# Keeping the first token block's x on chip, and 24 instead of 16 tiles with scores masked in PSUM, in a fused attention and two-MLP kernel

## The chip, the core and the metric

The kernel runs on one core of a Trainium2 chip. The metric is device time in microseconds (us) of one execution. The engines are TensorE (PE, matrix multiplications; PEld is its weight load), VectorE (DVE), ScalarE (ACT), GpSimd (POOL) and SyncE (SP, which issues the DMAs here). Each engine works through its own instructions in the order in which they were written.

## The reference

All inputs are float32. Attention has 4 batches, 8 heads, 576 tokens and 64 numbers for each head; the two MLPs then work on 2304 tokens of width 512.

```python
scores = (q @ k.T) / sqrt(64)
thresh = max(scores) - tau                     # for each row of scores
e = exp(where(scores >= thresh, scores, -1e9) - max(scores))
x = (e / (sum(e) + 1e-9)) @ v                  # (2304, 512) after the heads are put side by side
h = x @ w_in;  y = (h * sigmoid(h)) @ w_out    # 512 -> 2048 -> 512
out = ((y @ w_a) * (y @ w_b)) @ w_o            # 512 -> 1536 -> 512
```

## The kernel before

**Order of work.** The whole program is a list of tasks (`pl.add`), each with an engine, an estimated cost, a rank, the tasks that it needs, and the buffers that it takes (`take`) and gives back (`pl.free`). A list scheduler (`Plan.run`) plays the tasks through with the estimated costs and writes each engine's instructions in the order in which they start there. So the order is fixed when the kernel is built, by estimates; on the chip an instruction whose operands come late holds up everything behind it on its engine. A buffer ring such as `hb=1` has so many buffers, and its takers come in the order in which the tasks were added. Where the plan sees PE idle ahead of a transposition, `turn` puts in up to 16 transpositions that serve nothing else (L558).

**Attention.** Two heads are a pair (`c` = 0 to 3), and the queries of a batch come in two halves of 256 and 320 tokens. A tile is 128 query rows against all 576 keys. The first batch goes through all pairs with its first half (tiles 0 to 15, 4 for each pair), then through all pairs with its second half (tiles 16 to 35, 5 for each); the other batches follow. For each tile (`softmax`): PE computes the scores into a PSUM buffer, "sa" or "sb" (L502); DVE scales them and finds the extreme of each row (`lowest`, L511); a small DVE instruction makes the threshold; ACT takes the exponential (L523 or L525); DVE masks it and sums each row (`mask`, L528). `weigh` then turns the tile with PE transpositions in pieces of 128 columns (L560, into "tp" or "hb"), ACT copies them to SBUF (L567), and for each pair and half PE multiplies with `v` into the PSUM tile "av" (L605).

**Early tiles.** A tile with number below `EARLY` = 16 alternates between "sa" and "sb", its exponential and its mask read the scores from PSUM, and the buffer comes free with the mask. The transpositions of tiles below `EARLY - 2` use "hb" for every third piece of work. A later tile uses "sa" alone: `lowest` writes the scaled scores to SBUF as well (tile "t"), the exponential and the mask read "t", and "sa" comes free after `lowest`.

**The sums.** `inverses` adds a small number to the 4 or 5 columns of row sums (`guard`, L457) and takes their reciprocals (`inverse`, L460) into one shared tile "sums". PE transposes "sums" into the same "av" bank (`turn_sums`, L610). ACT copies both to SBUF (`evacuate`, L626, tile "x", ring of one). A DMA stores the inverse sums to DRAM (L630), a second one loads them back spread over the partitions (L637, "xi"), POOL multiplies (`divide`, L640), and a third DMA stores x to DRAM (L644).

**The MLPs.** The first MLP works on token blocks: five of 256 tokens, then two of 512. Block 0 is the first half of batch 0. `load_x` reads x of a block from DRAM for each pair (L694, "xr"), ACT rounds it to float32r (L699, "xh") and POOL takes the rest (L702, "xl"). `mlp1_up` and `mlp1_down` go over 16 chunks f of the inner width, PE in the order up(0), up(1), down(0), and so on. `up` accumulates in "hb" (L730), `down` of the first blocks in "sb" (L790); ACT and DVE apply the gate between them (L740, L743, L746, L749). Attention has the better rank on PE. The weights of the first MLP come in 32 chunks of 512 KB (L326), one for every 1.3 tiles; ACT, DVE and POOL split each one (L330, L335, L341, L346, L350, L354, L358). The second MLP follows (L876, L920).

Of the kernel before, what the change touches and what calls it, by code (L numbers as in the profile page):

```python
# [20 lines left out]
B, H, S, D = 4, 8, 576, 64  # L21
P = 128
# [9 lines left out]
TB = 256  # L32

BLOCKS = tuple((i * TB, TB) for i in range(5)) + ((5 * TB, 512), (5 * TB + 512, 512))
# [11 lines left out]
R_T, R_AV, R_EV, R_NORM = 2, 3, 1, -2  # L46
R_LD, R_SPLIT, R_AUX, R_MLP = -9, -6, -1, 1000

SPLIT_FROM = 54

EARLY = 16

AV_PARTS = ((0, 1, 2, 3), (4,))

# [6 lines left out]
PIECE = 128  # L61
# [153 lines left out]
def fused_kernel(ctx: ExitStack, tc: tile.TileContext, qk, qk2, v, tau, w_in, w_out, w_a, w_b, w_o2, out):  # L215
# [9 lines left out]
    nc = tc.nc  # L225
    pl = Plan()
# [8 lines left out]
    def pool(stack, name, bufs, side="left", **kw):  # L235
# [18 lines left out]
    xb_p = pool(p1, "xb", RINGS["xb"])  # L254
# [7 lines left out]
    x_p = pool(att, "x", RINGS["x"])  # L262
# [6 lines left out]
    sums = const.tile([P, P], F32, name="sums")  # L269
# [5 lines left out]
    ident = const.tile([P, P], F32, name="ident")  # L275
# [113 lines left out]
    att_tasks = []  # L389

    def add(engine, cost, rank, fn, after=(), take=(), behind=(), **kw):
        t = pl.add(engine, cost, rank, fn, after, take, behind, **kw)
        att_tasks.append(t)
        return t
# [51 lines left out]
        att_tasks.append(s["ready"])  # L446
        return s

    def inverses(n, m):

        s = {}

        def guard():
            nc.vector.tensor_scalar(out=s["sum"][:, :m], in0=s["sum"][:, :m], scalar1=EPS, scalar2=None, op0=ALU.add)  # L457

        def inverse():
            nc.vector.reciprocal(out=sums[:, :m], in_=s["sum"][:, :m])  # L460

        def total(k):
            def fn():
                if "sum" not in s:
                    s["sum"] = sm_p.tile([P, 5], F32, name="sum", bufs=2)
                return s["sum"][:, k:k + 1]
            return fn

        def finish(masked):
            gd = add("DVE", 150, n + R_NORM, guard, masked)  # L470
            return add("DVE", 150, n + R_NORM, inverse, [gd], ["rs"])

        return total, finish

    counter = [0]

# [69 lines left out]

    def weigh(b, half, c, tiles, v, last):

        q0, nq = HALVES[half]
        buf = "pb" if half else "pa"  # L550
        s = {}

# [15 lines left out]
            return fn  # L568

        left, full, es = [], [], []  # L570
        total, finish = inverses(counter[0] + len(tiles), len(tiles))

        def move(r, chunks, dst, *free):
            t = {"bank": "hb" if r < EARLY - 2 and turns[0] % 3 == 2 else "tp"}
# [13 lines left out]
        for n, parts in enumerate(tiles):  # L588
            e = softmax(parts, total(n))
            es.append(e)  # L590
            r = first + n
            tn = move(r, [(e, k * P) for k in range(4)], lambda p, n=n: p[:, :4, n * P:(n + 1) * P])
            if n % 2 or n == len(tiles) - 1:

                m = n % 2 + 1
                tn = move(r, [(x, S - P) for x in es[-m:]], lambda p, n=n, m=m: p[:, 4, (n + 1 - m) * P:(n + 1) * P])
                for _ in range(m):
                    pl.free("e", tn)
        last_n = first + len(tiles) - 1
# [7 lines left out]

        def turn_sums():
            s["av"] = ps_av.tile([P, 512], F32, name="av")
            nc.tensor.transpose(s["av"][:, nq:nq + P], sums, ident)  # L610

        iv = finish([e["ready"] for e in es])
        ts = add("PE", 110, last_n + R_AV, turn_sums, [iv], ["av"])
        pl.free("rs", ts)

        av = ts
        for ks in AV_PARTS:
            av = add("PE", 2 * len(ks) * (int(nq / 1.2) + 47) + 100, last_n + R_AV, lambda ks=ks: values(ks),
                     [*(left if 4 in ks else full), v["ready"]], behind=[av])
# [2 lines left out]
            pl.free("v", av)  # L622

        def evacuate():
            s["x"] = x_p.tile([P, 320 + P], F32, name="x")
            nc.scalar.copy(out=s["x"][:, :nq + P], in_=s["av"][:, :nq + P])  # L626

        def store_sums():
            k0 = 4 * half
# [7 lines left out]
            nc.sync.dma_start(out=s["i"][:, :nq], in_=r.broadcast_to((2, D, nq)))  # L637

        def divide(o):
            nc.gpsimd.tensor_tensor(out=s["x"][:, o], in0=s["x"][:, o], in1=s["i"][:, o], op=ALU.mult)  # L640

        def store():
            t0 = b * S + q0
            nc.sync.dma_start(out=xT_d[c, :, t0:t0 + nq], in_=s["x"][:, :nq])  # L644

        ev = add("ACT", act_ns(nq + P, True), last_n + R_EV, evacuate, [av], ["x"])
        pl.free("av", ev)
        st = dma(-1, 5 * P * 4, store_sums, after=[ev], slack=500)
        ld = dma(-1, P * 4 * nq, load_sums, after=[st], take=["xi"], slack=SLACK)
        dv = on_pool(nq, last_n + R_EV, divide, [ld], PIECE)  # L650
# [26 lines left out]
    xs, gs, ys = {}, {}, {}  # L677
    x_ready, g_ready, w_last = {}, {}, {}
    up_last, down_last, y_dma, b_done = [None], [None], [], []

    def load_x(j):
        s = xs[j] = {}
        t0, tn = BLOCKS[j]
        big = tn > TB
        x_p = lambda: pools["b5"] if big else xb_p
        ring, raw = ("x5", "xr5") if big else ("xb", "xr")

        def split(c):
            need = [t for (b, half, heads), ts in x_dma.items() for t in ts
                    if heads == c and b * S + HALVES[half][0] < t0 + tn and b * S + sum(HALVES[half]) > t0]  # L690

            def load():
                s["r", c] = x_p().tile([P, tn], F32, name=raw, bufs=RINGS[raw])
                nc.sync.dma_start(out=s["r", c], in_=xT_d[c, :, t0:t0 + tn])  # L694

            def hi():
                s["h", c] = x_p().tile([P, tn], F32R, name="xh5" if big else "xh", bufs=RINGS[ring])
                s["l", c] = x_p().tile([P, tn], F32R, name="xl5" if big else "xl", bufs=RINGS[ring])
                nc.scalar.copy(out=s["h", c], in_=s["r", c])  # L699

            def lo(o):
                nc.gpsimd.tensor_tensor(out=s["l", c][:, o], in0=s["r", c][:, o], in1=s["h", c][:, o].bitcast(F32), op=ALU.subtract)  # L702

            ld = dma(-1, P * 4 * tn, load, after=need, take=[raw], slack=SLACK, behind=[closed] if big else [])
            h = pl.add("ACT", act_ns(tn), R_AUX, hi, [ld], [ring])
            l = on_pool(tn, R_AUX, lo, [h], PIECE)[-1]
            pl.free(raw, l)
            x_ready[j, c] = (h, l)

        for c in range(NC):  # L710
            split(c)
# [260 lines left out]
    closed = pl.add("none", 1, 0, close_attention, behind=[*att_tasks, *closed0])  # L972
    units = [(j, f) for j in range(len(BLOCKS)) for f in range(NF)]
    for n, u in enumerate(units):
        if u[1] == 0:
            load_x(u[0])
        mlp1_up(n, *u)
        if n:
            mlp1_down(n - 1, *units[n - 1])
# [76 lines left out]
```

## Time and profile before

| | us |
|---|---|
| median of 3 runs | 1173.22 (1172.68 to 1173.97) |
| the profiled execution | 1174.95 |
| its span, first to last instruction | 1173.2 |
| PE busy in it | 1142.9 (97%) |
| DVE, ACT, POOL busy | 621.7, 531.1, 271.4 |

The span is what the rows below are taken from; the time of the same execution is 1.75 us above it. A busy time is the time in which an engine had an instruction in work; idle time in a row is the time the engine stood just before an instruction, and "<-" names what ended it. [...]

### The profile page before, as it was taken

The page shows a single profiled execution, that of the slowest core. Times are in us where ns is not written, and L with a number is a line of the kernel's source. Part 1 is how long each engine was busy: PE and PEld are TensorE (multiplying, and loading weights), DVE is VectorE, ACT ScalarE, POOL GpSimd, SP SyncE. Part 2 cuts the span into 40 slices and gives each one's busy share as a digit, 9 for nine tenths or more (in the row PEclk, how much of TensorE's full clock was granted, in tenths as well). Part 3 has the DMA queues.
Part 4 walks back from the last instruction along what each step waited for, and adds up shares of the span by engine and source line. Part 5 has one row for each costly group of instructions (what it writes and reads, how often), then busy time and mean ns, then how long its engine had stood idle before and what let it go on. Part 6 is the DMA issues. An engine that isn't in the chain of part 4 may idle for free.

```text
span 1173.2 us, 18253 instructions
## 1 busy us (share of the span) xinstructions
PE 1142.9 (97%) x6917; PEld 957.8 (82%) x6917; DVE 621.7 (53%) x1416; ACT 531.1 (45%) x999; POOL 271.4 (23%) x440
## 2 busy tenths in 40 slices
PE   8789989999999999999999999999999999999998
PEld 6456757988999989899888888888888888888897
DVE  8988887877777777463223678673211311211121
ACT  7877786666766766442223445442211211211121
POOL 2444444333322422140001344451000000000000
PEclk9999999999999999999999999999999999999999
DMA  6654543322322221150001235440100200000000
GB/s 199 199 163 138 163 155 109 113 88 79 107 73 84 82 95 35 36 190 18 1 1 45 88 111 167 140 138 13 63 1 1 68 0 1 23 28 1 1 36 18
DMA packets 41095, 90.05 MB, mean 77 GB/s; under 512 B 4256, under 2 KB 18224, under 8 KB 41008
## 3 DMA queue, kind: packets, MB, share of 16 engines
q1 hardware_dynamic: 40864, 88.89, 23.7%
q8 instruction: 54, 0.88, 0.3%
q14 instruction: 33, 0.27, 0.1%
q10 hardware_dynamic: 144, 0.00, 0.0%
HBM read 74.65 MB, written 14.23 MB: 76 GB/s over the span
## 4 chain that ended last, share of the span: by engine, by line
PE 60%; DMA 2%; DVE 1%; ACT 1%; issue 0%; POOL 0%; SPq 0%; ACTq 0%; POOLq 0%
PE ps_a L876 13%; PE op L920 13%; PE ps_b L876 13%; PE hb L730 5%; PE hc L730 4%; PE sb L790 3%; PE yc L790 2%; PE yd L790 1%; PE ye L790 1%; PE yf L790 1%; DMA wraw<-w_a 1%; PE av L605 1%; PE tp L560 1%; PE sa L495 1%; DMA wraw<-w_b 1%
## 5 line engine op out<-in xcount | busy, mean ns | idle before, releaser
L886 DVE TENSOR_TENSOR z<-ps_b,z 128x512 f32<-128x512 f32 (+1 forms) x60 | 38.2, 637 | 227.9 <-PE ps_b L876 227.8
L730 PE MATMUL hb<-xh,w 128*128 128x256 f32 (+1 forms) x704 | 155.2, 310 | 1.5 <-DVE th L743 1.0
L350 POOL TENSOR_TENSOR wt<-wc,wt 128x128 uint32<-128x128 uint32 (+1 forms) x164 | 111.2, 702 | 140.2 <-DVE wc L346 98.7
L920 PE MATMUL op<-w,zh 128*128 128x512 f32 x432 | 133.9, 391 | 0.0
L511 DVE TENSOR_SCALAR_CACHE_REDUCE t<-sa,nscale 128x576 f32<-128x576 f32 x128 | 103.7, 810 | 50.6 <-PE sa L495 45.6
L528 DVE SCALAR_TENSOR_TENSOR e<-t,thr,e 128x576 f32<-128x576 f32 x128 | 111.5, 871 | 26.4 <-ACT e L525 24.8
L730 PEld LDWEIGHTS hb<-xh,w 128*128 128x128 f32 x704 | 113.0, 190 | 10.9 <-issue 2.3
L560 PE MATMUL tp<-ident,e 128*128 128x128 f32 x706 | 106.2, 278 | 12.9 <-DVE e L528 8.3
L560 PEld LDWEIGHTS tp<-ident,e 128*128 128x128 f32 x706 | 78.7, 140 | 37.2 <-issue 14.7
L525 ACT ACTIVATE e<-t,min 128x576 f32<-128x576 f32 x128 | 99.9, 781 | 19.2 <-DVE t L511 18.5
L883 ACT COPY z<-ps_a 128x512 f32<-128x512 f32 (+1 forms) x60 | 32.6, 543 | 165.0 <-PE ps_a L876 165.0
L730 PE MATMUL hb<-xl,w 128*128 128x256 f32 (+1 forms) x352 | 106.5, 303 | 0.7 <-POOL xl L702 0.7
L790 PE MATMUL sb<-gh,w 128*128 128x256 f32 (+1 forms) x576 | 97.6, 300 | 0.0
L920 PEld LDWEIGHTS op<-w,zh 128*128 128x128 f32 x432 | 80.3, 188 | 16.4
L889 ACT CAST zh<-z 128x512 fp32r<-128x512 f32 (+1 forms) x60 | 34.7, 578 | 127.5 <-DVE z L886 127.5
L790 PEld LDWEIGHTS sb<-gh,w 128*128 128x128 f32 x576 | 80.0, 190 | 5.9 <-issue 3.3
L920 PE MATMUL op<-w,zl 128*128 128x512 f32 x216 | 84.6, 392 | 0.0
L749 DVE TENSOR_TENSOR gl<-th,gh 128x256 fp32r<-128x256 f32 (+1 forms) x112 | 63.9, 571 | 28.3 <-ACT gh L746 28.1
L876 PE MATMUL ps_a<-yha,w 128*128 128x512 f32 (+1 forms) x288 | 77.4, 355 | 0.0
L876 PE MATMUL ps_b<-yha,w 128*128 128x512 f32 (+1 forms) x288 | 77.0, 354 | 0.0
L640 POOL TENSOR_TENSOR x<-x,xi 128x128 f32<-128x128 f32 (+2 forms) x80 | 40.9, 535 | 147.1 <-issue 49.9
L702 POOL TENSOR_TENSOR xl<-xr,xh 128x128 fp32r<-128x128 f32 x72 | 37.0, 542 | 161.0 <-ACT xh L699 156.4
(123 smaller groups left out, 2342.8 us busy)
## 6 DMA issues: line engine op xcount, KB each, us to landing
qk<-qk SPq DMA_DIRECT2D x20, 576.0 KB
wraw<-w_in SPq DMA_DIRECT2D x16, 512.0 KB
wraw<-w_out SPq DMA_DIRECT2D x16, 512.0 KB
v<-v SPq DMA_DIRECT2D x20, 320.0 KB
wraw<-w_a SPq DMA_DIRECT2D x12, 512.0 KB
wraw<-w_b SPq DMA_DIRECT2D x12, 512.0 KB
wraw<-w_o SPq DMA_DIRECT2D x12, 512.0 KB
out<-ob SPq DMA_DIRECT2D x18, 256.0 KB
```

The source lines that it names most:

```text
L350: nc.gpsimd.tensor_tensor(out=s["t"][:, o], in0=s["c"][:, o].bitcast(U32), in1=s["t"][:, o], op=ALU.add)
L511: nc.vector.tensor_scalar(out=s["t"], in0=s["s"][:, :, :NH], scalar1=nscale, scalar2=None, op0=ALU.mult, op1=ALU.min, accum_out=s["min"])
L525: nc.scalar.activation(out=s["e"], in_=s["t"], func=AF.Exp, scale=-1.0, bias=s["min"])
L528: nc.vector.scalar_tensor_tensor(out=s["e"], in0=s["s"][:, :, :NH] if early else s["t"], scalar=s["thr"], in1=s["e"], op0=ALU.is_ge if ear ...
L560: nc.tensor.transpose(t["tp"][:, j * P:(j + 1) * P], e["e"][:, o:o + P], ident)
L640: nc.gpsimd.tensor_tensor(out=s["x"][:, o], in0=s["x"][:, o], in1=s["i"][:, o], op=ALU.mult)
L730: nc.tensor.matmul(s["h"], lhsT=w[:, a, o:o + P], rhs=xx, start=(c == 0 and k == 0), stop=(c == NC - 1 and k == 2))
L749: nc.vector.tensor_sub(out=s["gl"], in0=s["t"], in1=s["gh"].bitcast(F32))
L790: nc.tensor.matmul(ys[j][e // per][:, e % per * tn:(e % per + 1) * tn], lhsT=w[:, a, e * P:(e + 1) * P], rhs=gs[j, f][g], start=(f == 0 an ...
L876: nc.tensor.matmul(s[nm][:, :tn], lhsT=w[:, a, o:o + P], rhs=yy[:, :tn], start=(c == 0 and k == 0), stop=(c == NC - 1 and k == 2))
L886: nc.vector.tensor_mul(out=s["z"][:, :tn], in0=s["b"][:, :tn], in1=s["z"][:, :tn])
L920: nc.tensor.matmul(o_ps[t0, i], lhsT=s[z][:, i * P:(i + 1) * P], rhs=wt["o2", f][:, a, :], start=(f == 0 and k == 0), stop=(f == NF2 - 1 a ...
```

## The change

For the first half of batch 0 (`stays`), x no longer goes to DRAM and back.

- `inverse` takes the reciprocal of each sum 64 times over: DVE writes a tile of 128 x 4 x 64 numbers ("xi") from the 4 sums, read with a broadcast.
- `turn_sums` is four matmuls with a 128x64 weight from that tile and the identity, in place of one transposition. They put the inverse sums of 128 queries into 64 partitions each, beside the product with `v` in the "av" bank.
- `evacuate` copies 512 columns instead of 384, and `divide` reads the inverse sums from the same tile "x".
- The DMAs L630, L637, L644 and L694 of these four pairs are gone, and with them the buffer "xr". The split into "xh" and "xl" (now `split_x`) reads the tile "x" as soon as POOL has multiplied, and "x" comes free when the split is done.
- `EARLY` is 24: tiles 16 to 23 alternate between "sa" and "sb", keep their scores in PSUM until the mask, and write no tile "t"; transpositions of tiles 14 to 21 use "hb" for every third piece of work as well. "hb" and "sb" come to the first MLP after their last takers among these tiles.

```diff
-EARLY = 16
+EARLY = 24
...
-    def inverses(n, m):
+    def inverses(n, m, wide):
...
         def inverse():
-            nc.vector.reciprocal(out=sums[:, :m], in_=s["sum"][:, :m])
+            if wide:
+                s["wide"] = x_p.tile([P, 320], F32, name="xi")[:, :m * D].rearrange("p (m d) -> p m d", d=D)
+                nc.vector.reciprocal(out=s["wide"], in_=s["sum"][:, :m].rearrange("p (m o) -> p m o", o=1).broadcast_to((P, m, D)))
+            else:
+                nc.vector.reciprocal(out=sums[:, :m], in_=s["sum"][:, :m])
...
-            return add("DVE", 150, n + R_NORM, inverse, [gd], ["rs"])
+            return add("DVE", dve_ns(m * D) if wide else 150, n + R_NORM, inverse, [gd], ["xi" if wide else "rs"])
...
         q0, nq = HALVES[half]
+        stays = b == 0 and half == 0
...
         def turn_sums():
             s["av"] = ps_av.tile([P, 512], F32, name="av")
-            nc.tensor.transpose(s["av"][:, nq:nq + P], sums, ident)
+            if stays:
+                for k in range(4):
+                    nc.tensor.matmul(s["av"][k // 2 * D:(k // 2 + 1) * D, nq + k % 2 * P:][:, :P], lhsT=inv["wide"][:, k, :], rhs=ident,
+                                     start=True, stop=True, skip_group_check=True)
+            else:
+                nc.tensor.transpose(s["av"][:, nq:nq + P], sums, ident)
...
-        ts = add("PE", 110, last_n + R_AV, turn_sums, [iv], ["av"])
-        pl.free("rs", ts)
+        ts = add("PE", 450 if stays else 110, last_n + R_AV, turn_sums, [iv], ["av"])
+        pl.free("xi" if stays else "rs", ts)
...
         def evacuate():
-            s["x"] = x_p.tile([P, 320 + P], F32, name="x")
-            nc.scalar.copy(out=s["x"][:, :nq + P], in_=s["av"][:, :nq + P])
+            s["x"] = x_p.tile([P, 512], F32, name="x")
+            m = 2 * nq if stays else nq + P
+            nc.scalar.copy(out=s["x"][:, :m], in_=s["av"][:, :m])
...
         def divide(o):
-            nc.gpsimd.tensor_tensor(out=s["x"][:, o], in0=s["x"][:, o], in1=s["i"][:, o], op=ALU.mult)
+            nc.gpsimd.tensor_tensor(out=s["x"][:, o], in0=s["x"][:, o], in1=(s["x"][:, nq:] if stays else s["i"])[:, o], op=ALU.mult)
...
+        if stays:
+            dv = on_pool(nq, last_n + R_EV, divide, [ev], PIECE)
+            att_tasks.extend([*dv, *split_x(0, c, lambda: s["x"], dv[-1:], "x")])
+            return es
...
+    def split_x(j, c, src, after, held):
+        s = xs.setdefault(j, {})
+        t0, tn = BLOCKS[j]
+        big = tn > TB
+        ring = "x5" if big else "xb"
+        def hi():
+            p = pools["b5"] if big else xb_p
+            s["h", c] = p.tile([P, tn], F32R, name="xh5" if big else "xh", bufs=RINGS[ring])
+            s["l", c] = p.tile([P, tn], F32R, name="xl5" if big else "xl", bufs=RINGS[ring])
+            nc.scalar.copy(out=s["h", c], in_=src()[:, :tn])
+        def lo(o):
+            nc.gpsimd.tensor_tensor(out=s["l", c][:, o], in0=src()[:, o], in1=s["h", c][:, o].bitcast(F32), op=ALU.subtract)
+        h = pl.add("ACT", act_ns(tn), R_AUX, hi, after, [ring])
+        ls = on_pool(tn, R_AUX, lo, [h], PIECE)
+        pl.free(held, ls[-1])
+        x_ready[j, c] = (h, ls[-1])
+        return h, *ls
...
-        if u[1] == 0:
+        if u[1] == 0 and u[0]:
             load_x(u[0])
```

## Rows read from the trace of the kernel before

**Rows 1.** The page, part 1: busy time, share of the span, instructions of each engine.

```profile
PE 1142.9 (97%) x6917; PEld 957.8 (82%) x6917; DVE 621.7 (53%) x1416; ACT 531.1 (45%) x999; POOL 271.4 (23%) x440
```

**Rows 2.** Busy time by stretch: stretch, length, engines, mean clock, DMA share, GB/s.

```profile
16.00:47.00 31.00, 27.26 (x199) 17.39 (x197) 29.07 (x78) 26.49 (x48) 13.18 (x31) 1.00 0.64 202
47.00:65.00 18.00, 12.71 (x91) 7.66 (x87) 14.33 (x39) 13.57 (x27) 9.29 (x19) 1.00 0.61 190
65.00:80.00 15.00, 11.56 (x69) 6.37 (x69) 12.39 (x32) 11.58 (x22) 7.80 (x16) 0.89 0.53 171
80.00:140.00 60.00, 57.72 (x424) 44.54 (x423) 49.96 (x126) 44.45 (x92) 27.10 (x54) 1.00 0.48 150
140.00:200.00 60.00, 53.43 (x386) 39.02 (x385) 47.30 (x124) 43.45 (x85) 26.12 (x53) 0.97 0.44 135
200.00:550.00 350.00, 347.40 (x2815) 316.71 (x2814) 241.28 (x654) 215.06 (x426) 110.14 (x197) 1.00 0.26 84
```

**Rows 3.** Timeline of DVE: start, length, instruction, count, idle time before and its releaser.

```profile
27.38 0.82 DVE L528 SCALAR_TENSOR_TENSOR e<-sa,thr,e 128x576 f32<-128x576 f32 x1 [0.56 <-ACT e L523]
...
55.46 0.82 DVE L511 TENSOR_SCALAR_CACHE_REDUCE t<-sa,nscale 128x576 f32<-128x576 f32 x1 [0.98 <-PE sa L502]
...
60.64 0.82 DVE L528 SCALAR_TENSOR_TENSOR e<-t,thr,e 128x576 f32<-128x576 f32 x1 [1.60 <-ACT e L525]
...
75.00 0.82 DVE L511 TENSOR_SCALAR_CACHE_REDUCE t<-sa,nscale 128x576 f32<-128x576 f32 x1 [0.79 <-PE sa L502]
```

**Rows 4.** Timelines of PE, ACT, SP and POOL: pair 3 of block 0.

```profile
51.76 2.38 PE L605 MATMUL av<-pa,v 128*64 128x256 f32 x20
...
59.18 0.48 ACT L626 COPY x<-av 128x384 f32<-128x384 f32 x1 [1.30 <-DMA xT_d<-x]
...
70.67 0.37 SPq L694 DMA_DIRECT2D xr<-xT_d  x1
...
77.02 0.87 POOL L702 TENSOR_TENSOR xl<-xr,xh 128x128 fp32r<-128x128 f32 x2
...
77.94 0.39 PE L730 MATMUL hb<-xl,w 128*128 128x256 f32 x1 [0.69 <-POOL xl L702]
...
81.30 0.64 PE L790 MATMUL sb<-gh,w 128*128 128x256 f32 x4
```

**Rows 5.** Groups of DVE instructions, whole span: count, busy us, mean ns, idle before.

```profile
L460 DVE RECIPROCAL sums<-sum 128x5 f32<-128x5 f32 x16 | 2.9, 184 | 0.1
L460 DVE RECIPROCAL sums<-sum 128x4 f32<-128x4 f32 x16 | 2.8, 172 | 0.0
```

**Rows 6.** Groups of instructions from 0 to 182 us.

```profile
L528 DVE SCALAR_TENSOR_TENSOR e<-t,thr,e 128x576 f32<-128x576 f32 x34 | 30.4, 895 | 8.6 <-ACT e L525 7.6
L528 DVE SCALAR_TENSOR_TENSOR e<-sa,thr,e 128x576 f32<-128x576 f32 x8 | 6.5, 817 | 0.8 <-ACT e L523 0.6
L743 DVE SCALAR_TENSOR_TENSOR th<-th,hb 128x256 f32<-128x256 f32 x14 | 5.9, 420 | 5.1 <-ACT th L740 4.9
L567 ACT COPY pa<-tp 128x512 f32<-128x512 f32 x24 | 13.7, 586 | 0.7 <-PE tp L560 0.5
```

**Rows 7.** Timeline of PE: warm-up, the turned sums, transpositions of tile 21, two products with v.

```profile
1.05 3.80 PE L274 MATMUL av<-sums 128*128 128x128 f32 x18 [1.05 <-DVE back L293]
...
16.15 0.33 PE L610 MATMUL av<-ident,sums 128*128 128x128 f32 x1
...
69.08 4.60 PE L605 MATMUL av<-pb,v 128*64 128x320 f32 x20
73.61 0.66 PE L560 MATMUL tp<-ident,e 128*128 128x128 f32 x4
...
91.53 2.91 PE L605 MATMUL av<-pb,v 128*64 128x320 f32 x20
```

**Rows 8.** Busy time by stretch again, one microsecond around the slow product.

```profile
70.00:71.00 1.00, 1.00 (x6) 0.49 (x4) 1.00 (x4) 0.71 (x2) 0.71 (x2) 0.50 0.03 8
```

**Rows 9.** Waits of POOL, 47 to 80 us: total us, times, longest.

```profile
POOL wt L350 <- DVE wc L346: 4.4, 2, 2.6
```

More of the change, by code (lines that the diff above doesn't have):

```diff
@@ L470, in finish @@
             gd = add("DVE", 150, n + R_NORM, guard, masked)
-            return add("DVE", 150, n + R_NORM, inverse, [gd], ["rs"])
-        return total, finish
+            return add("DVE", dve_ns(m * D) if wide else 150, n + R_NORM, inverse, [gd], ["xi" if wide else "rs"])
+        return total, finish, s
     counter = [0]
@@ L570, in weigh @@
         left, full, es = [], [], []
-        total, finish = inverses(counter[0] + len(tiles), len(tiles))
+        total, finish, inv = inverses(counter[0] + len(tiles), len(tiles), stays)
         def move(r, chunks, dst, *free):
@@ L644, in store @@
             nc.sync.dma_start(out=xT_d[c, :, t0:t0 + nq], in_=s["x"][:, :nq])
-        ev = add("ACT", act_ns(nq + P, True), last_n + R_EV, evacuate, [av], ["x"])
+        ev = add("ACT", act_ns(2 * nq if stays else nq + P, True), last_n + R_EV, evacuate, [av], ["x"])
         pl.free("av", ev)
+        if stays:
+            dv = on_pool(nq, last_n + R_EV, divide, [ev], PIECE)
+            att_tasks.extend([*dv, *split_x(0, c, lambda: s["x"], dv[-1:], "x")])
+            return es
         st = dma(-1, 5 * P * 4, store_sums, after=[ev], slack=500)
@@ L679, in fused_kernel, with load_x @@
     up_last, down_last, y_dma, b_done = [None], [None], [], []
-    def load_x(j):
-        s = xs[j] = {}
+    def split_x(j, c, src, after, held):
+        s = xs.setdefault(j, {})
         t0, tn = BLOCKS[j]
         big = tn > TB
-        x_p = lambda: pools["b5"] if big else xb_p
-        ring, raw = ("x5", "xr5") if big else ("xb", "xr")
+        ring = "x5" if big else "xb"
[11 more added lines that the diff above has]
+        return h, *ls
+    def load_x(j):
+        s = xs.setdefault(j, {})
+        t0, tn = BLOCKS[j]
+        big = tn > TB
+        raw = "xr5" if big else "xr"
         def split(c):
@@ L692, in load @@
             def load():
-                s["r", c] = x_p().tile([P, tn], F32, name=raw, bufs=RINGS[raw])
+                s["r", c] = (pools["b5"] if big else xb_p).tile([P, tn], F32, name=raw, bufs=RINGS[raw])
                 nc.sync.dma_start(out=s["r", c], in_=xT_d[c, :, t0:t0 + tn])
[L696 to L702, printed above, removed]
             ld = dma(-1, P * 4 * tn, load, after=need, take=[raw], slack=SLACK, behind=[closed] if big else [])
[L705 to L708, printed above, removed]
+            split_x(j, c, lambda: s["r", c], [ld], raw)
         for c in range(NC):
```

## The prediction

> **What bounds the kernel now.** I read the page's first part, then the busy time by stretch, and inside the first stretches the timelines of DVE and PE. PE is busy 97% of the span [rows 1], so in most of the kernel time is PE work. The stretches show where it isn't [rows 2]. From 200 to 550 us PE is busy 347.4 of 350, and from 80 to 140 us 57.7 of 60: there PE is the bound, and a delay of other engines counts only as far as it leaves PE without work. From 16 to 47 us PE is idle for 3.7 of 31 us, part of its busy time being transpositions that serve nothing, while DVE is busy 29.07 of 31, or 94%. There DVE sets the pace. From 47 to 80 us neither is full: DVE 14.33 + 12.39 = 26.7 of 33 us, PE 24.3. DVE still sets the pace, with stops: it waits 0.98 and 0.79 us for scores in "sa", the only score buffer of late tiles, and 1.60 us for an exponential [rows 3]. That exponential stood on ACT behind a copy into "x" that waited 1.30 us until an earlier x had been stored [rows 4]. From 140 to 200 us PE is idle for 6.6 us while weights arrive chunk by chunk; their place is tied to the tiles.
>
> Block 0 of the first MLP is what PE could do in its idle time. Its last product with v begins at 51.76, and the matmul that needs that pair's rest, "xl", runs at 77.94, after a wait of 0.69 us [rows 4]. Between the two lie a copy, four DMAs and work of POOL and ACT. The first down matmul comes at 81.30, and only from there is PE full.
>
> **The change, part by part.** *The wide reciprocal (DVE, four times).* It replaces 128x4 at 172 ns by 128x256. The trace has no wide reciprocal. From below: an instruction of 256 columns that takes one column after the other is 420 ns [rows 6]. From above: the same instruction with a fifth column takes 184 instead of 172 ns [rows 5], so 12 ns a column, and 172 + 252 x 12 = 3.2 us. The slope is that of this very instruction, so I stay near it; but it is one column's difference of two means, and I take 2.5 us. Added: 4 x (2.5 - 0.17) = 9.3 us of DVE (bounds 1.0 and 12.1). The first three fall at about 15 to 41 us, where DVE is 94% busy, the fourth at 51 us. DVE's small idle pieces cover little: 0.56 us right behind the second one [rows 3], and I allow 1.0 in all. Behind each reciprocal DVE's masks and extremes wait, for these ACT and PE; PE's turned sums wait too, during the same time, so it counts once. DVE is 8.3 us late at tile 18.
>
> [...]
>
> *The four matmuls (PE, four times).* They replace a transposition of 0.33 us [rows 7]. From below: a product with v has 20 passes of 256 columns in 2.38 us [rows 4], 0.12 us each; 8 passes of half as many make 0.5 us. From above: the warm-up's 18 passes of 128x128 took 3.80 us [rows 7], so 8 take 1.7 us. I take 0.75, nearer to the product, which also fills half the columns of the array. That adds 1.7 us (0.7 to 5.5) where PE is idle for 12% of the time and waits for DVE: on the path nothing. Without that cover it costs its 1.7 us.
>
> *The copy of "av" (ACT, four times)*: 512 columns are 0.59 us [rows 6], 384 were 0.48 [rows 4]: 0.4 us in all on an engine busy 26.5 of 31 us, counted at nothing. *Divide and split*: the same POOL and ACT instructions, earlier.
>
> *The DMAs.* Sixteen issues leave SP's queue. Behind them stood loads of weights and q, k; those also wait for their buffers, which DVE frees, so I count nothing (at most a gain of 1 us). What does leave the path is ACT's wait of 1.30 us for the stored x.
>
> *Early tiles 16 to 23.* With two score buffers DVE's waits of 0.98 and 0.79 us go. The mask reads one operand from PSUM and takes 817 instead of 895 ns [rows 6]: 8 x 0.08 = 0.6 us. With ACT's 1.30 that is 3.7 us off the stretch from 47 to 80. [...] So DVE is 8.3 - 3.7 = 4.6 us late at tile 24.
>
> *The MLP's start.* x of the last pair is ready some 6 to 8 us after its product begins, not 26: the product 2.4, the copy 0.6, two pairs of POOL pieces at 0.87 [rows 4], the rounding between them, and the handovers. But "hb" comes free only when tile 21 is turned, which was at 73.61 [rows 7] and will be near 79, and "sb" after the mask of tile 23. So the MLP starts at about the same time as before, with attention three tiles less far: its work then fills idle time of PE among tiles 22 to 25. From 65 to 80 us PE was idle for 3.4 us [rows 2], and it ran a product with v in 4.60 us that later took 2.91 [rows 7], as the clock had gone to 0.50 [rows 8]: 1.7 more. Of these 5.1 us, 1.1 go to nine matmuls of block 0 (of 256 columns, at the 0.12 us of [rows 4]) that ran before 65 us and now come later. Of the remaining 4.0 I count half, 2.0, as "hb" opens in the middle of that stretch.
>
> **Sum.** 9.3 - 1.0 - 3.7 - 2.0 = +2.6 us. From 80 us on PE is full again and works off the same list. The profiled execution took 1174.95, 1.7 us above the median; the difference applies to either, and from the median it gives 1173.2 + 2.6 = 1175.8.
>
> **The rivals.** *The wide reciprocal costs what other DVE work of 256 columns costs* (faster). Then its term is +1.0 instead of 9.3 - 1.0, and the sum is 1.0 - 3.7 - 2.0 = -4.7: 1168.5. Against it speaks the 12 ns of a fifth column; for it, that this is a difference of 12 ns only. The point from which it decides: with r for its duration, 4 x (r - 0.17) - 1.0 equals 5.7 at r = 1.85 us.
>
> *PE's full stretch takes the delay up* (no change). From 80 to 140 us DVE is busy 83% [rows 2], so DVE, being late, can catch up while PE works on block 0, which by then is further on. If only what PE has lost counts, the 2.6 us shrink to nothing: 1173.2. For it speaks that PE bounds there; against it, that PE has to do the late attention as well, and that weights, which set the stretch from 140 us on, come with the tiles.
>
> *x lies ready and its buffer does not* (the change does not bring the earlier start). If the first up waits for "hb" until the tiles 22 and 23 are through as well, the 2.0 us are not had: 1177.8, and with 1.1 us for the nine moved matmuls 1178.9. For it speaks that "hb" has one buffer.
>
> *ACT waits for POOL.* The rounding of x stands in ACT's queue right behind POOL's multiplication, with no DMA's slack in between. POOL takes its work in order and stood up to 2.6 us in front of a weight piece for DVE [rows 9]. Four such waits on ACT, half of each passed on to DVE through the exponential, are +5.2: 1181.0. ACT's idle time there, 4.5 of 31 us, speaks against all of it counting.
>
> **How the numbers follow.** Chances: the forecast 0.35 (its own range 1174 to 1179), the cheap reciprocal 0.20, the delay taken up 0.25, the buffer not free 0.12, ACT behind POOL 0.08. The forecast is the likeliest: 1176. The bounds of the reciprocal alone move the sum from -4.7 to +5.4; with the last rival the cases reach from 1168.5 to 1181. Leaving out about 1 in 10 at each end, the range is 1168 to 1181. About 0.2%, 2.35 us, is what a measurement of this kernel can tell from no change, so faster is below 1170.9 and slower above 1175.5. Slower: 0.7 of the forecast and the last two rivals, 0.45. Faster: the cheap reciprocal and a third of the case taken up, 0.28. Same: 0.27.
>
> **What would show it.** L460 on 128x256 in the groups of DVE: 2 us or more, or 0.4. The scores of tile 16 come some 6 us later if the reciprocals are dear, and under 1 us later if they are cheap. L528 with "sa" and "sb" in the place of "t" eight more times at 0.82. The waits of DVE for "sa" between 47 and 80 us are gone, and so is ACT's for xT_d. The first up matmul comes right after tile 21 is turned, and the clock's stretch at 0.50 near 70 us is gone or has moved. From 200 us on PE is as full as before. The prediction is wrong if the reciprocal is short; if the tiles 16 to 23 gain much more than 3.7 us; or if the stretch from 140 to 200 us gets longer, since block 0 runs out of weights earlier than I count.

## The result and the profile after

The changed kernel takes 1180.47 us (median of 4 runs, 1178.12 to 1181.35), the kernel before 1173.6 beside it: ratio 1.0057, 95% interval [1.0039, 1.0075]. A second measurement gave 1.0037 [1.0024, 1.0050]. So the change costs 0.4 to 0.6%, 4 to 7 us. The forecast was 1176, slower.

The page of the changed kernel's profile, part 1, and its busy time by stretch, in the columns of [rows 1, 2] (the profiled execution took 1180.23 us, its span 1178.4):

```profile
PE 1144.4 (97%) x6968; PEld 961.3 (82%) x6968; DVE 628.2 (53%) x1416; ACT 530.1 (45%) x999; POOL 274.7 (23%) x440
...
16.00:47.00 31.00, 25.18 (x200) 16.43 (x198) 30.09 (x71) 23.69 (x43) 13.56 (x31) 1.00 0.51 155
47.00:65.00 18.00, 13.55 (x110) 8.93 (x106) 14.93 (x36) 13.83 (x27) 8.26 (x20) 1.00 0.55 173
65.00:80.00 15.00, 13.40 (x91) 8.90 (x92) 13.70 (x35) 12.90 (x26) 6.59 (x14) 1.00 0.47 147
80.00:140.00 60.00, 57.08 (x429) 43.72 (x428) 51.31 (x130) 45.67 (x95) 27.80 (x51) 1.00 0.51 159
140.00:200.00 60.00, 52.73 (x376) 39.38 (x375) 47.69 (x122) 42.06 (x82) 27.21 (x54) 0.94 0.44 133
200.00:550.00 350.00, 344.23 (x2790) 312.51 (x2791) 242.31 (x656) 214.71 (x427) 112.81 (x197) 1.00 0.26 84
```

Three things stand against [rows 2]. From 16 to 47 us DVE is busy 30.09 us instead of 29.07, now 97%, and it gets through 71 records instead of 78, PE being idle for 5.8 instead of 3.7 us. From 47 to 80 us PE is fuller: 26.95 instead of 24.27 us. That isn't more work: of it 5.36 us are 41 of the plan's transpositions that serve nothing (called fillers below), where the kernel before had 7 in 1.37 us. From 200 to 550 us, where PE had been idle for 2.6 us, it is idle for 5.8.

Groups of DVE, first 190 us (count, busy us, mean ns, idle before), and the timeline of PE (start, length), then that of the kernel before:

```profile
L462 DVE RECIPROCAL xi<-sum 128x256 f32<-128x256 f32 x4 | 7.0, 1750 | 0.0
L532 DVE SCALAR_TENSOR_TENSOR e<-sb,thr,e 128x576 f32<-128x576 f32 x12 | 9.8, 814 | 1.6 <-ACT e L527 1.4
L532 DVE SCALAR_TENSOR_TENSOR e<-sa,thr,e 128x576 f32<-128x576 f32 x12 | 9.7, 808 | 2.5 <-ACT e L527 2.4
```

```profile
42.92 0.66 PE L621 MATMUL av<-ident,xi 128*64 128x128 f32 x8 [1.29 <-DVE xi L462]
...
48.90 0.65 PE L506 MATMUL sa<-qk 64*128 64x288 f32 x4
...
57.22 0.66 PE L621 MATMUL av<-ident,xi 128*64 128x128 f32 x8 [2.06 <-DVE xi L462]
...
60.56 0.72 PE L506 MATMUL sa<-qk 64*64 64x288 f32 x8
...
73.31 3.32 PE L613 MATMUL av<-pb,v 128*64 128x320 f32 x20
...
78.59 0.76 PE L506 MATMUL sa<-qk 64*128 64x288 f32 x4
79.28 0.50 PE L759 MATMUL hb<-xh,w 128*128 128x256 f32 x2
```

```profile
46.55 0.76 PE L502 MATMUL sa<-qk 64*128 64x288 f32 x4
...
54.65 0.72 PE L502 MATMUL sa<-qk 64*64 64x288 f32 x8
...
75.88 0.76 PE L502 MATMUL sa<-qk 64*128 64x288 f32 x4 [0.39 <-DVE t L511]
```

A wide reciprocal takes 1.75 us, and PE stands 1.2 to 2.1 us in front of the four matmuls, which need 0.66 us. The three score lines of each kernel are those of tiles 16, 18 and 24, so attention is 2.4, then 5.9, and by tile 24 only 2.7 us late (most at tile 20, 66.58 and 58.84 us). The first MLP starts at 79.28 us.

At 120 us the changed kernel and the kernel before have done the same: 95 and 96 matmul records of "up", 72 and 73 of "down", 140 of products with v each, 156 of scores each. The loss is made after that. At 450 us the changed kernel has 636 and 612 records of up and down, the kernel before 654 and 636.

### The profile page after: what moved, and what is told of

It is laid out like the page before. It is cut to its first block, busy times and chain, and to the rows that moved or that the text cites. A ratio compares the mean times of both kernels' runs of the same rounds, so it can differ in the third digit from the quotient of the medians.

```text
span 1178.4 us, 18332 instructions
## 1 busy us (share of the span) xinstructions
PE 1144.4 (97%) x6968; PEld 961.3 (82%) x6968; DVE 628.2 (53%) x1416; ACT 530.1 (45%) x999; POOL 274.7 (23%) x440
## 4 chain that ended last, share of the span: by engine, by line
PE 60%; DMA 1%; ACT 0%; issue 0%; DVE 0%; POOL 0%; ACTq 0%
PE ps_a L905 13%; PE op L949 13%; PE ps_b L905 13%; PE hb L759 5%; PE hc L759 4%; PE sb L819 3%; PE yf L819 2%; PE ye L819 2%; PE yc L819 2%; PE yd L819 2%; DMA yr<-yT_d 1%; PE av L613 1%; PE tp L568 1%; PE sa L499 1%; ACT yha L879 0%; DMA xT_d<-x 0%
## 5 line engine op out<-in xcount | busy, mean ns | idle before, releaser
L515 DVE TENSOR_SCALAR_CACHE_REDUCE t<-sa,nscale 128x576 f32<-128x576 f32 x120 | 97.3, 811 | 45.8 <-PE sa L499 41.9
L532 DVE SCALAR_TENSOR_TENSOR e<-t,thr,e 128x576 f32<-128x576 f32 x120 | 105.0, 875 | 20.6 <-ACT e L529 19.4
L529 ACT ACTIVATE e<-t,min 128x576 f32<-128x576 f32 x120 | 93.4, 780 | 21.6 <-DVE t L515 21.1
L772 DVE SCALAR_TENSOR_TENSOR th<-th,hb 128x256 f32<-128x256 f32 (+1 forms) x88 | 40.9, 465 | 59.5 <-ACT th L769 58.7
L655 POOL TENSOR_TENSOR x<-x,xi 128x107 f32<-128x107 f32 (+2 forms) x72 | 37.1, 539 | 146.8 <-DMA xi<-r_d 77.1
```

Source lines behind the costliest of these rows:

```text
L515: nc.vector.tensor_scalar(out=s["t"], in0=s["s"][:, :, :NH], scalar1=nscale, scalar2=None, op0=ALU.mult, op1=ALU.min, accum_out=s["min"])
L529: nc.scalar.activation(out=s["e"], in_=s["t"], func=AF.Exp, scale=-1.0, bias=s["min"])
L532: nc.vector.scalar_tensor_tensor(out=s["e"], in0=s["s"][:, :, :NH] if early else s["t"], scalar=s["thr"], in1=s["e"], op0=ALU.is_ge if ear ...
L772: nc.vector.scalar_tensor_tensor(out=s["t"], in0=s["t"], scalar=1.0, in1=s["h"], op0=ALU.add, op1=ALU.mult)
```

## The experiments

In the table, idle is the length of a stretch less PE's busy time in it, from one profile for each kernel (the changed kernel's two profiles differ by up to 1.7 us); fillers count as busy; the clock is the median over a kernel's timed runs of the mean granted TensorE clock, with full speed as 1. The last column multiplies each run's time with its clock and takes the median; differences in it are good to about 1 us. It is the author's rough estimate of the time without what moments at a lower clock cost (in the changed kernel four score matmuls took 1.33 us at 162 us, where the clock was 0.50, and 0.76 at 171 us, where it was 1.00), and by the same estimate too low by what waits take during them. The three measurements of the kernel before give 1170.0, 1170.0 and 1169.9 by it.

| kernel | ratio to before, 95% interval | PE idle 0-120 | 120-200 | 200-550 | clock | time x clock |
|---|---|---|---|---|---|---|
| before | 1 | 16.9 | 6.9 | 2.6 | 0.994-0.996 | 1170.0 |
| changed | 1.0057 [1.0039, 1.0075] | 14.3 | 10.2 | 5.8 | 0.996 | 1175.6 |
| r_after, the same again | 1.0037 [1.0024, 1.0050] | 12.7 | 9.0 | 5.5 | 0.9965 | 1175.7 |
| e1_before_wide | 1.0020 [1.0004, 1.0035] | 17.3 | 5.8 | 1.4 | 0.9945 | 1172.6 |
| e2_after_cheap | 1.0009 [0.9995, 1.0023] | 10.6 | 10.9 | 4.8 | 0.996 | 1172.9 |
| e3_stay_only | 1.0057 [1.0035, 1.0078] | 14.6 | 13.9 | 1.5 | 0.994 | 1175.7 |
| e4_early_only | 0.9980 [0.9962, 0.9999] | 15.6 | 4.1 | 3.5 | 0.997 | 1170.4 |
| e5_stay_cheap | 1.0032 [1.0020, 1.0045] | 10.9 | 13.3 | 3.8 | 0.993 | 1172.9 |
| e6_early_wide | 1.0019 [1.0006, 1.0032] | 18.0 | 4.6 | 3.9 | 0.997 | 1175.4 |
| e7_weight_broadcast | 0.9964 [0.9949, 0.9979] | 10.3 | 7.1 | 3.3 | 0.9955 | 1167.8 |
| e8_after_no_wide | 1.0027 [1.0014, 1.0040] | 10.0 | 12.0 | 3.2 | 0.996 | 1172.5 |
| e9_wide_cost150 | 1.0013 [1.0000, 1.0025] | 15.5 | 7.3 | 3.6 | 0.996 | 1171.8 |
| e10_cost1750 | 1.0065 [1.0051, 1.0079] | 15.3 | 8.2 | 5.9 | 0.994 | 1177.3 |
| e11_broadcast_16 | 0.9990 [0.9977, 1.0003] | 11.9 | 10.1 | 2.3 | 0.999 | 1173.9 |

### The reciprocals alone, the early tiles alone

**e1_before_wide** is the kernel before, its order kept, with four wide reciprocals into a tile of 128 x 4 x 64 that nobody reads (1722 ns each).

```diff
...
             nc.vector.reciprocal(out=sums[:, :m], in_=s["sum"][:, :m])
+            if wide:
+                nc.vector.reciprocal(out=spare, in_=s["sum"][:, :m].rearrange("p (m o) -> p m o", o=1).broadcast_to((P, m, D)))
...
```

> The kernel before, with one more instruction: behind each of the four narrow reciprocals of block 0 a wide one, 128x256, into a tile that nobody reads. The order on all engines is that of before. It adds 4 x 1.75 us to DVE, and nothing else. Theory A (the wide reciprocals cost time because DVE sets the pace where they stand, and what they cost early is not won back): 1178 to 1180, that is 5 to 7 us above before. Theory B (the delay is taken up by the stretch from 80 to 140 us, where PE is full; the change loses its time behind 120 us, through the order that the plan wrote there): within 2 us of before, 1172 to 1176.

1.0020: the reciprocals alone make the kernel before 2.4 us slower, less than theory A's 5 to 7 and a little more than theory B's 2. At 120 us the profiled execution is 4 to 5 us back (84 instead of 96 records of up, 64 instead of 73 of down); part of it is made up later. Not all of that need be the reciprocals' own time: the mean clock of its first 120 us is 0.94, that of the kernel before 0.99, and PE was busy for 150 ns a matmul record there, 142 in the kernel before.

**e2_after_cheap** is the changed kernel in its own order, the wide reciprocal replaced by a narrow one (168 ns) and a copy that spreads it (360 ns in the mean: three of 0.3 us and one of 0.56).

```diff
-                nc.vector.reciprocal(out=s["wide"], in_=s["sum"][:, :m].rearrange("p (m o) -> p m o", o=1).broadcast_to((P, m, D)))
+                nc.vector.reciprocal(out=s["sum"][:, :m], in_=s["sum"][:, :m])
+                nc.vector.tensor_copy(out=s["wide"], in_=s["sum"][:, :m].rearrange("p (m o) -> p m o", o=1).broadcast_to((P, m, D)))
```

> The changed kernel with a narrow reciprocal, 128x4, and a broadcasting DVE copy to 128x256 in the place of the wide reciprocal; the plan's cost is left as it is, so the order on all engines stays that of the changed kernel. It takes 4 x about 1.2 us off DVE. Theory A: 1174 to 1176, the changed kernel less 4 to 6 us. Theory B: 1179 to 1182, like the changed kernel.

1.0009, 1.1 us above before. Theory A's 1174 to 1176 were 0.4 to 2.4 us above the 1173.6 known then, so it holds here: less DVE time helps. But the kernel isn't faster than before.

**e3_stay_only** is the changed kernel with 16 early tiles, as below; **e4_early_only** is the kernel before with 24, the same edit the other way round.

```diff
-EARLY = 24
+EARLY = 16
```

> The changed kernel with 16 early tiles: x of block 0 stays on chip, with its wide reciprocals, and the buffers hb and sb come free for the first MLP after tiles 13 and 15, as before. Theory A: the reciprocals cost their 6 us and the MLP, which can start some 10 us earlier, gives 2 to 4 back: 1175 to 1178. Theory B: the time is set by the order behind 120 us and can lie on either side; no early delay is seen at 120 us. If holding hb and sb is what costs in the change, this is 1168 to 1172.

> The kernel before with 24 early tiles and x through DRAM as before: no wide reciprocals, and hb and sb held until tiles 21 and 23. Theory A: the two score buffers give their 3.7 us and nothing takes them: 1168 to 1171. Theory B: whatever the order behind 120 us makes of it, 1173 or more; if the early tiles are what costs, 1178 to 1181.

e4 is faster by 0.2% [0.9962, 0.9999]. By time x clock nothing is left of that (1170.4 beside 1170.0), so it may be no more than fewer moments at a lower clock. Theory A had 2.6 to 5.6 us; it is 2.4. e3 is as slow as the whole change, 6.7 us above before, where theory A had 1.4 to 4.4. Its MLP does begin early, at 52 us, and PE pays from 120 us on. The stretches of e3:

```profile
80.00:120.00 40.00, 38.67 (x293) 29.58 (x294) 34.34 (x90) 30.67 (x61) 17.27 (x32) 1.00 0.55 163
120.00:140.00 20.00, 14.38 (x95) 11.34 (x94) 13.72 (x38) 13.73 (x29) 7.02 (x17) 0.94 0.55 159
140.00:200.00 60.00, 51.69 (x355) 35.96 (x353) 46.79 (x118) 41.93 (x83) 28.51 (x54) 0.93 0.39 117
```

From 120 to 200 us PE is idle for 5.6 + 8.3 = 13.9 us, before for 6.9. Block 0 needs its weights, and the early start brought them hardly sooner: the 20th of the 32 chunks was split at 126 us before and at 123 in the changed kernel and in e3, the last at 199, 201 and 199. That the weights are what PE lacks is inferred from this. Of the 13.9 us only 2.1 are direct waits of PE for a weight; 4.7 are waits for a mask and 4.3 for ACT's copies, in front of transpositions.

### The same work in other orders

The plan writes the order from estimates, so each edit of a cost also moves other work. The next kernels part the two.

**r_after** is the changed kernel once more, as a measure for the others.

> The changed kernel itself, so that it stands beside the next three on one chip. It was at a ratio of 1.0057 to the kernel before (1.0039 to 1.0075): 1.004 to 1.007 again.

1.0037, just under what was expected; time x clock is the same, 1175.7 and 1175.6.

**e5_stay_cheap** is e3 with the narrow reciprocal and the copy of e2; **e6_early_wide** is e4 with the four unread reciprocals of e1, its order kept.

> x of block 0 on chip, 16 early tiles, and a narrow reciprocal with a broadcasting copy in the place of the wide one; the order is that of the version with 16 early tiles and wide reciprocals, which was at 1.0057. Theory C (the wide reciprocals cost about 2 to 5 us in any order): 1.001 to 1.004. Theory D (with 16 early tiles the first MLP starts near 52 to 69 us, uses up block 0 and then stands still for want of weights from 120 to 200 us, and that is what costs): 1.004 or more, with PE idle from 120 to 200 us for over 12 us, as it was (14.2).

> 24 early tiles, x through DRAM, and four more wide reciprocals into a tile that nobody reads, in the order of the version with 24 early tiles alone (0.9980). Theory C: 0.9980 plus 0.002 to 0.005: 1.000 to 1.003. If on-chip x costs something of its own beside the reciprocals, this lies below the changed kernel by that: 1.000 to 1.003 against 1.0057. If on-chip x is free, it equals the changed kernel, 1.005 to 1.006.

e5 stays slow (1.0032) with PE idle for 13.3 us from 120 to 200: the cheaper reciprocal gains before 120 us (10.9 us idle instead of 14.6), and the later idle time remains, as theory D had it; the ratio is what theory C had. e6 loses 0.4% against e4, as theory C had it. It lies below the changed kernel by its ratio (1.0037 beside it) but not by time x clock (1175.4 and 1175.7), so what x on chip costs by itself isn't settled by it.

**e7_weight_broadcast** needs neither the wide reciprocal nor the copy. The reciprocal stays 128x4, and each of the four matmuls reads one column of it 64 times as its weight. The plan's cost of the reciprocal becomes 150 ns again, it writes to "sums" as before the change, and the order becomes another one.

```diff
...
-            return add("DVE", dve_ns(m * D) if wide else 150, n + R_NORM, inverse, [gd], ["xi" if wide else "rs"])
+            return add("DVE", 150, n + R_NORM, inverse, [gd], ["rs"])
...
-                    nc.tensor.matmul(s["av"][k // 2 * D:(k // 2 + 1) * D, nq + k % 2 * P:][:, :P], lhsT=inv["wide"][:, k, :], rhs=ident,
+                    nc.tensor.matmul(s["av"][k // 2 * D:(k // 2 + 1) * D, nq + k % 2 * P:][:, :P], lhsT=sums[:, k:k + 1].broadcast_to((P, D)), rhs=ident,
                                      start=True, stop=True, skip_group_check=True)
...
```

> The changed kernel with 24 early tiles, but no wide reciprocal and no copy: the reciprocal stays 128x4, and each of the four matmuls loads one column of it 64 times over as its weight. The plan's cost for it is 150 as before the change, so the order may differ a little from the changed kernel's. DVE has less to do than in any version with x on chip. Theory C: 0.999 to 1.001, the level of the version with a copy (1.0009) or 1 to 2 us better. If on-chip x brings the gain that it lacks there, 0.996 to 0.998, below the 24 early tiles alone (0.9980).

0.9964 [0.9949, 0.9979]: 4.2 us faster than before, the only one that clearly is. Its timeline of PE:

```profile
37.10 0.66 PE L617 MATMUL av<-ident,sums 128*64 128x128 f32 x8
37.58 2.33 PE L609 MATMUL av<-pa,v 128*64 128x256 f32 x20
```

The matmuls take the same 0.66 us as with a full weight, and PE waits for DVE in front of them for 1.7 us in the four places together, not 6.1.

e7 differs from e2 by 1.44 us of DVE and by its order, but by 0.0045 of the time, 5.3 us. So either small DVE costs are very dear, or the order counts. **e8_after_no_wide** takes the broadcast weight into the changed kernel's own order, each instruction in its place; **e9_wide_cost150** puts the wide reciprocal into e7's order.

The edit of e8, in the changed kernel:

```diff
-                s["wide"] = x_p.tile([P, 320], F32, name="xi")[:, :m * D].rearrange("p (m d) -> p m d", d=D)
-                nc.vector.reciprocal(out=s["wide"], in_=s["sum"][:, :m].rearrange("p (m o) -> p m o", o=1).broadcast_to((P, m, D)))
+                s["wide"] = x_p.tile([P, 320], F32, name="xi")
+                nc.vector.reciprocal(out=s["wide"][:, :m], in_=s["sum"][:, :m])
...
-                    nc.tensor.matmul(s["av"][k // 2 * D:(k // 2 + 1) * D, nq + k % 2 * P:][:, :P], lhsT=inv["wide"][:, k, :], rhs=ident,
+                    nc.tensor.matmul(s["av"][k // 2 * D:(k // 2 + 1) * D, nq + k % 2 * P:][:, :P], lhsT=inv["wide"][:, k:k + 1].broadcast_to((P, D)), rhs=ident,
```

and that of e9, in the changed kernel too:

```diff
-            return add("DVE", dve_ns(m * D) if wide else 150, n + R_NORM, inverse, [gd], ["xi" if wide else "rs"])
+            return add("DVE", 150, n + R_NORM, inverse, [gd], ["xi" if wide else "rs"])
```

> The changed kernel with every instruction of every engine in its own order, but the wide reciprocal of 128x256 (1.75 us, four of them) replaced by one of 128x4, and the spreading over the 64 partitions left to the four matmuls, whose weight is one column of it read 64 times. So 4 x 1.58 = 6.3 us go from VectorE and nothing else moves. Theory A (VectorE's time for the wide reciprocals is what the change lost): ratio 0.9955 to 0.9985. Rival B (the order that the plan works out, in which the reciprocal and the AV matmuls stand elsewhere, is what it lost): 0.999 to 1.003, since the order is kept.

> The kernel with the broadcast weight (ratio 0.9964) in its own order, but with the wide reciprocal of 128x256 back in front of its four matmuls. Theory A: four times 1.58 us on VectorE, of which the runs so far lost between 0.0020 and 0.0039 of the time: 0.9985 to 1.0010. Rival B (order alone): 0.995 to 0.998, as without the wide reciprocals.

Neither theory alone holds. By theory A e8 should have come to 0.9955 to 0.9985; it is at 1.0027. By rival B e9 should have been at 0.995 to 0.998; it is at 1.0013. Both count. Busy time from 0 to 120, 120 to 200 and 200 to 550 us, first e8, then e7, then e9:

```profile
0.00:120.00 120.00, 110.02 (x789) 77.89 (x789) 100.63 (x268) 94.14 (x176) 51.55 (x111) 0.97 0.55 166
120.00:200.00 80.00, 68.04 (x495) 50.07 (x491) 63.34 (x159) 55.24 (x111) 35.37 (x69) 0.98 0.46 136
200.00:550.00 350.00, 346.78 (x2809) 314.38 (x2810) 243.40 (x657) 214.43 (x426) 112.05 (x197) 1.00 0.26 84
```

```profile
0.00:120.00 120.00, 109.74 (x792) 76.37 (x793) 102.44 (x274) 95.39 (x178) 52.92 (x114) 0.97 0.58 175
120.00:200.00 80.00, 72.87 (x525) 53.68 (x525) 62.77 (x160) 58.47 (x116) 36.16 (x71) 0.98 0.42 128
```

```profile
0.00:120.00 120.00, 104.54 (x759) 72.52 (x760) 104.20 (x266) 92.50 (x173) 49.45 (x108) 0.99 0.54 165
120.00:200.00 80.00, 72.66 (x519) 54.20 (x520) 63.60 (x164) 57.80 (x115) 34.24 (x71) 0.96 0.46 140
```

Before 120 us PE's idle time goes with the reciprocals: 10.0 and 10.3 us without them (e8, e7), 14.3, 12.7 and 15.5 with them (changed, again, e9). From 120 to 200 us it seems to go with the order: 9.0 to 12.0 us in the four traces with the changed kernel's order, 7.1 and 7.3 in the two with e7's. But each order has its own number of fillers. PE's busy time with fillers alone, first the changed kernel, then e7 (e8 and e9 have the same counts, the kernel before 67 and 24):

```profile
0.00:120.00 120.00, 13.23 (x99) 10.61 (x99) 1.00 0.52 166
120.00:200.00 80.00, 3.00 (x14) 2.20 (x14) 0.96 0.44 135
```

```profile
0.00:120.00 120.00, 10.29 (x76) 8.15 (x76) 0.97 0.58 175
120.00:200.00 80.00, 4.92 (x32) 3.46 (x32) 0.98 0.42 128
```

With the fillers counted as idle, 12.0 to 14.2 us from 120 to 200 stand against 12.1 and 12.3, and about a third of that difference is left. So the idle columns compare kernels of one order only. What was done by then is seen in the matmuls themselves: the end of the seventh product with v, in the changed kernel, e8, e7 and e9.

```profile
110.10 2.91 PE L613 MATMUL av<-pb,v 128*64 128x320 f32 x20
```

```profile
109.04 2.91 PE L613 MATMUL av<-pb,v 128*64 128x320 f32 x20
```

```profile
105.62 0.76 PE L609 MATMUL av<-pb,v 128*64 128x320 f32 x4
```

```profile
111.28 0.76 PE L613 MATMUL av<-pb,v 128*64 128x320 f32 x4
```

It ends at 113.0, 112.0, 106.4 and 112.0 us, and at 120 us the records of up and down are 95 and 72, 96 and 72, 105 and 85, 89 and 72. So the order counts before 120 us as well: only e7, with the other order and without the reciprocals, is ahead there by over 5 us; e8 and e9 gain 1 in the products with v and nothing in up and down. (These are single profiles, and the mean clock of these 120 us is 1.00, 0.97, 0.97 and 0.99. In e2, which has e8's order with the copy and a clock of 1.00, the product ends at 110.2.) How much of the order's price are its fillers stays open: no run took them out.

In the changed kernel's order the stops stand at the same instructions with the reciprocals and without. Around 127 us, timelines of ACT, DVE and PE, first the changed kernel, then e8:

```profile
126.61 0.66 ACT L330 ACTIVATE wt<-wraw 128x512 uint32<-128x512 uint32 x1 [2.93 <-DMA wraw<-w_out]
...
127.84 0.42 DVE L772 SCALAR_TENSOR_TENSOR th<-th,hb 128x256 f32<-128x256 f32 x1 [3.61 <-ACT th L769]
...
128.32 0.51 PE L759 MATMUL hb<-xh,w 128*128 128x256 f32 x2 [1.50 <-DVE th L772]
...
186.39 0.33 PE L624 MATMUL av<-ident,sums 128*128 128x128 f32 x1 [2.54 <-DVE sums L464]
```

```profile
125.86 0.66 ACT L330 ACTIVATE wt<-wraw 128x512 uint32<-128x512 uint32 x1 [2.85 <-DMA wraw<-w_out]
...
127.09 0.42 DVE L772 SCALAR_TENSOR_TENSOR th<-th,hb 128x256 f32<-128x256 f32 x1 [3.53 <-ACT th L769]
...
127.57 0.50 PE L759 MATMUL hb<-xh,w 128*128 128x256 f32 x2 [1.42 <-DVE th L772]
...
183.94 0.47 PE L624 MATMUL av<-ident,sums 128*128 128x128 f32 x1 [2.66 <-DVE sums L464]
```

ACT's queue has the first step on a weight chunk (L330) ahead of the gate's "th" (L769). The chunk's DMA was issued at 119.17 us and lands 7.4 us later. ACT waits for it, DVE waits for ACT's "th", PE for DVE's, and no wide reciprocal is near. The other stop shown, before L624, is no mark of this order alone: the kernel before has one of 2.2 us there, e7 and e9 have 0.4 and 0.3. The splits of the 20th and 21st weight chunk on DVE, first in the changed kernel, then in the kernel before:

```profile
122.06 0.68 DVE L358 TENSOR_TENSOR w<-wt,w 128x512 fp32r<-128x512 f32 x1
132.28 0.69 DVE L358 TENSOR_TENSOR w<-wt,w 128x512 fp32r<-128x512 f32 x1
```

```profile
125.40 0.71 DVE L358 TENSOR_TENSOR w<-wt,w 128x512 fp32r<-128x512 f32 x1 [0.56 <-ACT w L354]
131.46 0.69 DVE L358 TENSOR_TENSOR w<-wt,w 128x512 fp32r<-128x512 f32 x1
```

They lie 10.2 us apart here, 9.4 to 10.1 in the other three traces of this order, 6.1 before and 5.1 in e7 and e9. The changed kernel is 3.3 us ahead of the kernel before at the 20th chunk and 0.8 to 4.5 us behind from the 21st to the last. Nor does e8's 4.3 us less idle time before 120 us mean as much work: its mean clock there is 0.97, and PE was busy for 139 ns a matmul record, 135 in the changed kernel at 1.00; and it has 1.8 us more idle time from 120 to 200.

**e10_cost1750** tells the plan the measured price of the wide reciprocal.

```diff
-            return add("DVE", dve_ns(m * D) if wide else 150, n + R_NORM, inverse, [gd], ["xi" if wide else "rs"])
+            return add("DVE", 1750 if wide else 150, n + R_NORM, inverse, [gd], ["xi" if wide else "rs"])
```

> The changed kernel with the plan told the measured price of its wide reciprocal (1750 ns in place of 333), so that the order is worked out anew. Theory A: the 6.3 us of VectorE stay, so 1.001 to 1.006. Rival B (the plan's wrong price put the work in a bad order): 0.996 to 1.000.

1.0065, just above theory A's range: the right price gives no better order (the slowest by its median, with an interval that overlaps the changed kernel's). So the changed kernel isn't slow because the plan misjudged the reciprocal (333 ns); a truer estimate doesn't make the order better by itself.

**e11_broadcast_16** is e7 with 16 early tiles.

```diff
-EARLY = 24
+EARLY = 16
```

> The kernel with the broadcast weight, x of the first block on chip, but 16 early tiles in place of 24. If x on chip alone is a gain: below 0.998. If the early start of the MLP is given back between 120 and 200 us, because the first block then runs out of weights: 0.999 to 1.003, with TensorE idle for 11 us or more from 120 to 200 us, as in the two runs with 16 early tiles before.

0.9990: x on chip with no DVE cost is worth nothing clear alone. PE is idle for 10.1 us from 120 to 200, less than the 11 expected and 2.9 more than in e7. The 24 early tiles, with the order that goes with them, add 0.26% here; the two intervals touch.

## Why the prediction was right, and where not

The direction was right, and 1180.5 lies in the range, but 4.5 above the forecast and outside the forecast's own range of 1174 to 1179. The range reaches that far only by the last rival, ACT behind POOL, which the trace doesn't show. Its steps:

- **The wide reciprocal: mis-sized.** 1.75 us, not 2.5, so 4 x (1.75 - 0.17) = 6.3 us and not 9.3. The slope is (1750 - 172) / 252 = 6.3 ns a column, half the 12 ns that the fifth column suggested. What these 6.3 us cost depends on the order. In six pairs that differ by them (e1 and before, e6 and e4, e9 and e7, changed and e8; e3 and e5, changed and e2 by 4.9, for the copy) the ratio moves by 0.0010 to 0.0049, and time x clock by 2.6, 5.0, 4.0, 3.1, 2.8 and 2.7 us. So 40 to 80% of the DVE time reached the end; the prediction let 8.3 of 9.3 us through.
- **The four matmuls**: 0.66 us for 0.75, right. The price is the wait for DVE, 6.1 us of PE in the four places, which the prediction counted once with DVE's delay.
- **Copy, divide, DMAs at nothing, and ACT's wait for the stored x gone**: nothing in the traces speaks against it. The wait for "xT_d" is gone.
- **Early tiles**: masks at 808 and 814 ns beside 893 from "t" in the same stretch, as [rows 6] had it. These are means: the medians are 817 and 821, but 12 of the 27 from "t" took 0.85 to 1.10 us and none of the 24 from PSUM over 0.82; why, no run shows. DVE's waits for "sa" from 47 to 80 us are down to one of 0.4. The delay of the scores rises to 7.7 us at tile 20 and falls to 2.7 at tile 24, by 5.0; the prediction had 8.3 and 4.6, by 3.7. Alone, in e4, the early tiles were worth 2.4 us, with an interval from 0.1 to 4.5, and nothing by time x clock.
- **The MLP's start**: 79.28, predicted near 79, right after tile 21 was turned. The clock from 65 to 80 us is 1.00, and the product with v took 3.32 instead of 4.60 us. PE is idle for 1.6 instead of 3.4 us there, but not because block 0 fills the gap, as the 2.0 us of the sum had it: 2.08 us are fillers, where the kernel before had none, and by 80 us 6 records of up have begun, not 17. The delay is made good from 80 to 120 us, where PE is busy for 40.00 us of 40 instead of 38.01.
- **"From 80 us on PE is full again and works off the same list": this step failed.** With the measured reciprocal the prediction's own sum is 6.3 - 1.0 - 3.7 - 2.0 = -0.4 us, no change. At 120 us that fits: the same work is done (the 2.6 us less idle time are fillers). Then PE loses 3.3 us from 120 to 200 (10.2 idle for 6.9; 2.6 with the fillers counted as idle) and 3.2 from 200 to 550. The prediction named it, as the third thing that would make it wrong, and gave it no time. Its two misses, an overpriced reciprocal and an unpriced order, had opposite signs, and it is by that luck that the direction came out right.

Of the loss, the reciprocals are some 3 us by time x clock (changed 1175.6, e8 1172.5); by the ratio it is 0.0010 to 0.0030, with intervals that overlap. What the order costs shows against e7's, the best one measured. Without reciprocals it is 4.7 us (e8 against e7, 1172.5 and 1167.8), with them 3.8 (changed against e9, 1175.6 and 1171.8). The prediction's rivals: the cheap reciprocal came about by size, 1.75 being under its point of 1.85 us, but not by time; the delay was taken up by 120 us and lost again; "hb" was free in time; ACT's waits for POOL from 16 to 80 us come to 1.2 us, all in front of weights.

Three things stay open: which of the plan's shifts makes this order slower (no run moved a single instruction), how much of it are the fillers (they don't decide alone: e4 has 123 in all and is no slower than the kernel before with 91, the changed kernel 114), and where the 3.2 us from 200 to 550 us come from: a kernel in the same order without the reciprocals has 0.6 there (e8), the one with the copy 2.2 (e2).

## What to carry to other kernels

Spreading a few numbers over many partitions cost no time of its own where the matmul read its weight with a broadcast (0.66 us for the four, as with a full weight); done by a reciprocal of every copy (1.75 us), on the engine that sets the pace, it used up the gain (e7 0.9964, e9 1.0013). An earlier start of a later stage can be given back: e3 began the MLP at 52 us and stood more from 120 us on (13.9 us up to 200 us, before 6.9), for want of weights as far as can be inferred. PE's busy time says nothing of work done while a kernel has instructions that serve nothing; count the matmuls that do. Where a plan writes the order, measure an edit in more than one order: the same instructions came out 0.2 to 0.6% apart.

## What the hardware showed beside that

The wide reciprocal took 1750 ns for 256 columns, the narrow one 172 for 4: 6.3 ns for each column more that it writes, though both read the same 4; a copy with the same broadcast took 360 ns in the mean for 256 columns, three of four 0.3 us. A weight read as one column 64 times cost no more than a full one, 0.66 us for eight passes of 128 columns in both. Moments at a lower clock wander: from 160 to 165 and from 165 to 170 us the changed kernel's clock is 0.64 and 0.68, while the dip of [rows 8] near 70 us is gone (1.00 from 65 to 80 us). The mean over an execution went from 0.991 to 1.000 among the runs, as wide a span as that of the ratios studied here.
